# One quadrant product of each expert layer by seven products of quarters, sums kept in PSUM, and GpSimd's transfers moved and spaced

## The chip, the cores and the metric

The kernel runs on one core of a Trainium2 chip. The metric is device time in microseconds of one execution, the median of several runs. Engines are named as in the profile: PE is TensorE (PEld its weight loads), DVE VectorE, ACT ScalarE, POOL GpSimd, SP SyncE, which issues most DMAs.

## The reference

All is fp32. A thresholded attention over 8 batches, 8 heads, 576 positions, head size 64 is followed by a mixture of 8 experts (512 to 1024 to 512) in which a hash of the token's id chooses the one expert:

```python
scores = scale * np.matmul(q, k.transpose(0, 1, 3, 2))
thresh = np.max(scores, axis=-1, keepdims=True) - tau
scores = np.where(scores >= thresh, scores, -1e9)
scores = scores - np.max(scores, axis=-1, keepdims=True)
attn = np.exp(scores); attn /= np.sum(attn, axis=-1, keepdims=True) + 1e-09
x = np.matmul(attn, v)          # (B,H,S,D) -> (B*S, H*D) = (4608, 512)
expert_idx = token_ids * 2654435761 % 8
for e in range(8):
    xe = x[expert_idx == e]
    out[expert_idx == e] = np.maximum(xe @ w1[e], 0.0) @ w2[e]
```

## The kernel before

**Attention.** 32 pairs of heads, each in five steps (`n = 5 p + s`, s from 0 to 4), written out as one order for all engines in a loop over `n`. A step scores a block of queries (L235, PE), negates it and takes the row maximum (`ns`, L246, DVE), gets `thr` from it (L253, POOL), exponentiates (L260, ACT), masks the block of the step before (L271, DVE), turns the weights (L282, PE, copied by ACT at L303) and multiplies with v (L313, PE). In step 0 the output of a pair is turned back (`turn_o`), divided (`put_xm`, L352, DVE) and written to `x_scratch` by SP. Routing is done on the side: once every token has a slot, 36 scatters (`scatters`, L542, POOL) write the table of slots, one in each step but s = 1. From step n = 131 on `fetch_early` gathers rows of x for the first expert (L119, POOL), one at the head of each step 0 and one at the end of steps 3 and 4, 15 in all.

**Experts.** Expert e has `caps[e]` slots: 544 for the first, 576 for experts 1 to 4, 600 from 5 on. Each layer is a product of 2 x 2 blocks done by seven products in place of eight (`seven`): with a the weights and b the activations, c11 = a11 b11 + a12 b21, and five more products of sums (s1 to s4 of a, t1 to t4 of b) give c12, c21 and c22. The sums are made by DVE (`left`, `right`, L858 and L861). Layer 1 runs in two groups of columns (g = 0, 1), layer 2 in one. A product goes to one of four PSUM tiles of two banks in turn (`bank2`: names `sc` and `bank`), and DVE adds it to the running sums p1, u2, u3, u4 in SBUF; ACT copies p1 and applies the ReLU (L948). In layer 2 of all experts but the last the columns of w2 are dealt out (`dealt`): weights are read with a step of four elements. A matmul in fp32 is two instructions in the trace.

Calls of `side1` and `side2` between the products place other work: sums of the next layer and expert (`w2_work`, `h_work`, `x_work`), transposes of the next expert's x (`turns`, L1056, DVE, then 16 DMAs of SP into `xT`), the gathers for expert e + 2 (`fetch`), the loads of its weights (2 MB each, SP), and `put_squares`, which turns half of an expert's output into `o_q` (L1028, DVE) and writes it with 8 to 10 indirect DMAs (L1036, POOL). The last expert is written by `put_out` and `last_tile`. Engines take their instructions in the order written; a loop over overflow tokens at the end runs no round with these inputs.

Of the kernel before, what the change touches and what calls it, by code (L numbers as in the profile page):

```python
# [9 lines left out]
FP32 = mybir.dt.float32  # L10
# [10 lines left out]
def kernel(  # L21
# [122 lines left out]
    with tc.tile_pool(name="a_q", bufs=1) as a_q, \  # L144
# [543 lines left out]
        with tc.manual_schedule():  # L688
# [21 lines left out]
            for n in range(LAST + NS + 1):  # L710
                p, s = divmod(n, NS)
                m = n - 2
                if s == 0:
                    fetch_early(n)
# [85 lines left out]
                if s != 1 and placed:  # L800
                    next(scatter_pieces, None)
                if s > 2:
                    fetch_early(n)
# [23 lines left out]
    with tc.tile_pool(name="m_x", bufs=1) as m_x, \  # L827
         tc.tile_pool(name="m_o", bufs=3) as m_o, \
# [9 lines left out]
        o_end = m_x.tile([P, DIN], FP32, name="o_end")  # L838
# [4 lines left out]
        w2_s = m_s.tile([P, 3, FH, D2], FP32, name="w2_s")  # L843
        h_s = m_s.tile([P, 3, FH, CH], FP32, name="h_s")
        halves = [m_s.tile([P, 2, CH], FP32, name=n) for n in ("p1", "u2", "u3", "u4")]
# [3 lines left out]
        turn = [0]  # L849

        def bank2():
            turn[0] ^= 1
            if turn[0]:
                return ps_sc.tile([P, 2, 512], FP32, name="sc")
            return ps_m.tile([P, 2, 512], FP32, name="bank2")
# [31 lines left out]
        def w2_sums(e):  # L887
            t = triple(w2_s, 0, FH)
            return t if e == E - 1 else [dealt(x, C2) for x in t]
# [19 lines left out]
        def sums_w2(e):  # L909
            s1 = None  # L910
            if e == E - 1:
                spare = w_pool.tile([P, CO, F], FP32, name="w1_sb")
                s1 = w_tiles["s1"] = spare[:, :, 0:D2]
            return left(*w2_blocks(e, w_tiles[e, 2]), w2_sums(e), s1)
# [11 lines left out]
        def seven(a, a_s, b, b_s, m0, outs, relu, after):  # L926

            (a11, a12, s1, a22), (s2, s3, s4) = a, a_s
            (b11, t1, b21, b22), (t2, t3, t4) = b, b_s
            c11, c12, c21, c22 = outs  # L930
            n_k, width, dealt_out = a11.shape[1], b11.shape[2], len(a11.shape) == 4
            p1, u2, u3, u4 = (t[:, :, 0:width] for t in halves)

            def product(x, y):
                ps = bank2()
                for i in range(2):
                    c0 = m0 + P * i
                    for c in range(n_k):
                        lhsT = (x[:, c, :, i] if dealt_out else
                                x[:, c, c0:c0 + P])  # L940
                        nc.tensor.matmul(ps[:, i, 0:width], lhsT=lhsT, rhs=y[:, c],  # L941
                                         start=c == 0, stop=c == n_k - 1)
                return ps[:, :, 0:width]
# [253 lines left out]
```

## Time and profile before

| | |
|---|---|
| median of 6 runs | 938.46 us (936.81 to 942.33) |
| profiled execution | 940.78 us |
| its span, first to last instruction | 939.2 us |
| mean granted PE clock | 0.993 |
| attention / experts, about | 0 to 480 / 500 to 931 us |
| DMA traffic | 113.11 MB, mean 120 GB/s |

A group's line in the profile is: line, engine, operation, out<-in by the program's names, shapes, count | busy us, mean ns of one | idle time of the engine just before them and what ended it. "remote" or "another core or an unknown queue" stands where no instruction of the profile explains the end of a wait. PE's ends are modelled, since matmuls overlap; the distance between starts is what counts. Times of other kernels in this document stand against these runs.

### The profile page before, as it was taken

The page shows a single profiled execution, that of the slowest core. Times are in us where ns is not written, and L with a number is a line of the kernel's source. Part 1 is how long each engine was busy: PE and PEld are TensorE (multiplying, and loading weights), DVE is VectorE, ACT ScalarE, POOL GpSimd, SP SyncE. Part 2 cuts the span into 40 slices and gives each one's busy share as a digit, 9 for nine tenths or more (in the row PEclk, how much of TensorE's full clock was granted, in tenths as well). Part 3 has the DMA queues.
Part 4 walks back from the last instruction along what each step waited for, and adds up shares of the span by engine and source line. Part 5 has one row for each costly group of instructions (what it writes and reads, how often), then busy time and mean ns, then how long its engine had stood idle before and what let it go on. Part 6 is the DMA issues. An engine that isn't in the chain of part 4 may idle for free.

```text
span 939.2 us, 20725 instructions
## 1 busy us (share of the span) xinstructions
PE 914.6 (97%) x7495; PEld 664.4 (71%) x7495; DVE 757.9 (81%) x1654; ACT 457.2 (49%) x741; POOL 403.2 (43%) x528
## 2 busy tenths in 40 slices
PE   8999999999999999999999999999999999989996
PEld 4666666656666666565678887798888878768685
DVE  8999999999999999999756767768677786776551
ACT  6888888888888889888702020111102021020110
POOL 4233433456666532464325361716446171621602
PEclk9999999999999999999999999999999999999999
DMA  7355354454456667752103844363463626311101
GB/s 180 87 143 135 97 143 117 114 145 101 103 128 175 160 149 196 206 129 52 28 25 80 266 109 143 109 191 123 114 208 95 182 91 190 127 47 27 48 0 54
DMA packets 114775, 113.11 MB, mean 120 GB/s; under 512 B 32475, under 2 KB 89315, under 8 KB 114672
## 3 DMA queue, kind: packets, MB, share of 16 engines
q1 hardware_dynamic: 105168, 92.64, 37.4%
q0 software_dynamic: 9072, 18.91, 7.0%
q8 instruction: 61, 1.00, 0.5%
q14 instruction: 42, 0.34, 0.1%
q10 hardware_dynamic: 432, 0.21, 0.1%
HBM read 81.99 MB, written 21.44 MB: 110 GB/s over the span
## 4 chain that ended last, share of the span: by engine, by line
PE 68%; issue 18%; POOL 5%; DVE 2%; ACT 2%; DMA 2%; SPq 1%; another core or an unknown queue 1%; POOLq 0%; DVEq 0%; ACTq 0%
PE av L313 18%; PE sc L235 15%; PE tr L282 11%; PE bank L941 10%; PE sc L941 10%; POOL out_dram L1036 5%; PE sc L640 2%; PE av L282 1%; DMA xT<-xq 1%; ACT w L260 1%; ACT wT_b L303 1%; DMA k_sb<-in_k_dram 1%; POOL xg L119 1%; DVE ns L246 0%
## 5 line engine op out<-in xcount | busy, mean ns | idle before, releaser
L260 ACT ACTIVATE w<-ns,nmx 128x576 f32<-128x576 f32 x288 | 220.4, 776 | 29.6 <-DVE ns L246 29.1
L271 DVE SCALAR_TENSOR_TENSOR w<-ns,thr,w 128x576 f32<-128x576 f32 x288 | 225.4, 815 | 0.0
L1036 POOL DMA_INDIRECT out_dram<-o_q,qidx x127 | 136.9, 1078 | 198.6 <-DVE o_q L1028 159.9
L246 DVE TENSOR_SCALAR_CACHE_REDUCE ns<-sc 128x576 f32<-128x576 f32 x288 | 205.7, 747 | 8.8 <-PE sc L235 7.8
L253 POOL TENSOR_SCALAR thr<-nmx,drop 128x2 f32<-128x2 f32 (+1 forms) x160 | 103.1, 644 | 187.8 <-DVE ns L246 177.7
L235 PE MATMUL sc<-k_sb,q 64*128 64x288 f32 (+1 forms) x1280 | 178.9, 424 | 0.7 <-DVE drop L704 0.2
L282 PEld LDWEIGHTS tr<-ident,w 64*128 64x128 f32 x2624 | 105.5, 138 | 96.7 <-ACT wT_b L303 34.2
L282 PE MATMUL tr<-ident,w 64*128 64x64 f32 x2624 | 139.2, 230 | 7.2 <-ACT wT_b L303 4.3
L948 ACT ACTIVATE h<-h 128x576 f32<-128x576 f32 (+1 forms) x56 | 38.8, 693 | 172.0 <-DVE h L861 138.9
L235 PEld LDWEIGHTS sc<-k_sb,q 64*128 64x128 f32 (+1 forms) x1280 | 92.4, 177 | 23.7 <-DVE ns L246 9.6
L313 PE MATMUL av<-wT_a,v 128*64 128x320 f32 (+1 forms) x704 | 100.4, 418 | 0.2
L303 ACT COPY wT_a<-tr 128x512 f32<-128x512 f32 (+1 forms) x128 | 81.6, 638 | 20.9 <-PE tr L282 20.4
L303 ACT COPY wT_b<-tr 128x512 f32<-128x512 f32 (+1 forms) x128 | 81.3, 635 | 16.9 <-PE tr L282 9.6
L313 PE MATMUL av<-wT_b,v 128*64 128x256 f32 x640 | 83.2, 389 | 0.0
L313 PEld LDWEIGHTS av<-wT_a,v 128*64 128x64 f32 x704 | 43.7, 136 | 28.9 <-DVE xm L352 0.4
L951 ACT COPY p<-bank 128x576 f32<-128x576 f32 (+2 forms) x11 | 7.0, 632 | 98.7 <-PE bank L941 73.1
L313 PEld LDWEIGHTS av<-wT_b,v 128*64 128x64 f32 x640 | 40.2, 136 | 18.8 <-issue 0.7
L542 POOL DMA_INDIRECT slot_scratch<-tok,slot_i x36 | 45.2, 1255 | 9.8 <-issue 7.6
L941 PE MATMUL bank<-h,w_sb 128*128 128x288 f32 (+3 forms) x192 | 48.1, 404 | 0.0
L941 PE MATMUL sc<-h,w_sb 128*128 128x288 f32 (+3 forms) x192 | 47.7, 401 | 0.0
L941 PEld LDWEIGHTS bank<-h,w_sb 128*128 128x128 f32 x192 | 46.6, 300 | 0.5
L941 PEld LDWEIGHTS sc<-h,w_sb 128*128 128x128 f32 x192 | 45.9, 289 | 0.7
(197 smaller groups left out, 1314.7 us busy)
## 6 DMA issues: line engine op xcount, KB each, us to landing
w_sb<-in_moe_w_dram SPq DMA_DIRECT2D x16, 2048.0 KB
q<-in_q_dram SPq DMA_DIRECT2D x62, 288.0 KB
v<-in_v_dram SPq DMA_DIRECT2D x32, 256.0 KB
x_scratch<-xm SPq DMA_DIRECT2D x32, 256.0 KB
xT<-xq SPq DMA_DIRECT2D x84, 80.0 KB
k_sb<-in_k_dram SPq DMA_DIRECT2D x31, 144.0 KB
k_sb<-in_k_dram SPq DMA_DIRECT2D x32, 112.0 KB
x_scratch<-xg SPq DMA_DIRECT2D x9, 256.0 KB
```

The costliest lines, as they stand in the source:

```text
L235: nc.tensor.matmul(sc[out_rows, i, 0:S2], lhsT=q_sb[rows, h, q0:q1], rhs=k_sb[rows, h], start=True, stop=True)
L246: nc.vector.tensor_scalar(out=ns[:].rearrange("p (i s) -> p i s", i=2), in0=sc[:, :, 0:S2], scalar1=-1.0, scalar2=None, op0=ALU.mult, op1= ...
L253: nc.gpsimd.tensor_scalar(out=thr[:, 0:j + 1], in0=stats[n][0][:, 0:j + 1], scalar1=drop[:], scalar2=None, op0=ALU.add)
L260: nc.scalar.activation(w, nss[n, j][:], AF.Exp, bias=stats[n][0][:, j:j + 1], scale=-1.0)
L271: nc.vector.scalar_tensor_tensor(out=w, in0=nss.pop((n, j))[:], scalar=stats[n][1][:, j:j + 1], in1=w, op0=ALU.is_le, op1=ALU.mult, accum_ ...
L282: nc.tensor.transpose(dst[:, r, 64 * c:64 * c + 64], src[rows, c0:c0 + P], ident[rows, rows])
L303: nc.scalar.copy(dst, tr[:, :, 0:64 * n_c].rearrange("p r (c q) -> p r c q", c=n_c))
L313: nc.tensor.matmul(av[64 * j:64 * j + 64, g, c0:c1], lhsT=v_sb[:, c, 64 * j:64 * j + 64], rhs=wT[g][:, i, c0:c1], start=(c == 0), stop=stop)
L542: nc.gpsimd.indirect_dma_start(out=slot_dram[c % 2][:, :], out_offset=bass.IndirectOffsetOnAxis(ap=slot_i[:, c:c + 1], axis=0), in_=tok[:, ...
L941: nc.tensor.matmul(ps[:, i, 0:width], lhsT=lhsT, rhs=y[:, c], start=c == 0, stop=c == n_k - 1)
L948: nc.scalar.activation(c, c, AF.Relu)
L1036: inst = nc.gpsimd.indirect_dma_start(out=rows[:, :], out_offset=bass.IndirectOffsetOnAxis(ap=idx, axis=0), in_=o_sb, in_offset=None, boun ...
```

## The change

Three edits, all below in the diff.

1. In both layers of experts 1 to 7, a12 b21 is no longer computed as one block product but again by seven products of quarters (`Quarters`, operands from `w_quarters`, `b_quarters`, sums `wi_s`, `bi_s` made by `inner_w` and `inner_b`, w2's quarter copied to a packed tile by ACT in `copy_quarters`). Its products have half the columns, 144, 150 or 120.
2. The running sums p1, u2, u3 are accumulated in PSUM (`products` with `start=False`) on four fixed tiles (`banks`); ACT copies out the partial sums that are needed again. `Seven` and `Quarters` replace `seven`; `layer1` and `layer2` write the order of products out, and the side work is dealt to it by tables. `s4` of layer 2 is made in place. `put_squares(0, 0)` moves from layer 2 of expert 0 to layer 1 of expert 1, and the first half of later experts to the end of layer 2.
3. GpSimd's transfers: the scatters stand in attention steps 0 to 3 and the early gathers in 1 to 3; in the experts every write of `put_squares` and every gather after expert 1's is followed by `pause`, two copies of a 128 x 152 table.

The output tiles `o_sb` and `o_end` become the gather tiles `xg`. The diff, cut:

```diff
-                if s == 0:
-                    fetch_early(n)
...
-                if s != 1 and placed:
+                if s < NS - 1 and placed:
                     next(scatter_pieces, None)
-                if s > 2:
+                if 0 < s < NS - 1:
                     fetch_early(n)
                 if n == LAST:
...
-        w2_s = m_s.tile([P, 3, FH, D2], FP32, name="w2_s")
+        w2_s = m_s.tile([P, 2, FH, D2], FP32, name="w2_s")
+        w2_q = m_s.tile([P, 4, 2, P], FP32, name="w2_q")
-        halves = [m_s.tile([P, 2, CH], FP32, name=n) for n in ("p1", "u2", "u3", "u4")]
+        halves = [m_s.tile([P, 2, CH], FP32, name=n) for n in ("p1", "u2", "u3")]
+        wi_s = m_s.tile([P, 3, D2], FP32, name="wi_s")
+        bi_s = m_s.tile([P, 3, CH], FP32, name="bi_s")
+        quarters = [m_s.tile([P, CH], FP32, name=n) for n in ("q_p1", "q_u2", "q_p5")]
...
+        def bank2():
+            turn[0] += 1
+            return banks[(turn[0] - 1) % 4]
...
+            t = [w2_s[:, i] for i in range(2)]
+            if e == E - 1:
+                return [*t, w_tiles["s4"]]
+            return [*(dealt(x, C2) for x in t), w2_blocks(e, w_tiles[e, 2])[1]]
...
-        def seven(a, a_s, b, b_s, m0, outs, relu, after):
...
+        def products(ps, x, y, start, mid=None):
+            for i, lhsTs in enumerate(x):
+                for c, lhsT in enumerate(lhsTs):
+                    nc.tensor.matmul(ps[:, i], lhsT=lhsT, rhs=y[:, c], start=start and c == 0,
+                                     stop=c == len(lhsTs) - 1, skip_group_check=not start)
+                if i == 0 and mid:
+                    mid()
...
+            def first(self):
+                products(self.x, self.a[0], self.b[0], True)
+            def keep_p1(self):
+                nc.scalar.copy(self.p1, self.x)
+            def second(self, y):
+                y = y[:, :, 0:self.x.shape[2]]
+                products(y, self.a[1], self.b[2], True)
+                self.out(self.outs[0], y, self.p1)
+            def u2_sum(self):
+                products(self.x, self.a[4], self.b[4], False)
+                nc.scalar.copy(self.u2, self.x)
+            def s1_t1(self, keep):
+                products(self.z, self.a[2], self.b[1], True)
+                if keep:
+                    nc.scalar.copy(self.mid, self.z)
+            def u3_sum(self, keep):
+                products(self.x, self.a[5], self.b[5], False)
+                if keep:
+                    nc.scalar.copy(self.mid, self.x)
+            def c21(self):
+                products(self.x, self.a[3], self.b[6], False)
+                if self.relu:
+                    nc.scalar.activation(self.outs[2], self.x, AF.Relu)
+                else:
+                    nc.scalar.copy(self.outs[2], self.x)
+            def c12(self, mid=None):
+                products(self.z, self.a[6], self.b[3], False, mid)
+                self.out(self.outs[1], self.z, self.u2)
+            def c22(self, ps):
+                self.out(self.outs[3], ps, self.mid)
+            def c11(self, p1):
+                self.out(self.outs[0], p1, self.outs[0])
+        class Quarters:
...
+            def p1_p2(self):
+                products(self.x, self.a[0], self.b[0], True)
+                nc.scalar.copy(self.p1, self.x)
+                products(self.y, self.a[1], self.b[2], True)
+            def c11(self):
+                add(self.outs[0], self.y, self.p1)()
+            def p5_u2(self):
+                products(self.z, self.a[2], self.b[1], True)
+                nc.scalar.copy(self.p5, self.z)
+                products(self.x, self.a[4], self.b[4], False)
+                nc.scalar.copy(self.u2, self.x)
+            def c12_c22(self):
+                products(self.z, self.a[6], self.b[3], False)
+                add(self.outs[1], self.z, self.u2)()
+                products(self.x, self.a[5], self.b[5], False)
+                add(self.outs[3], self.x, self.p5)()
+            def c21(self):
+                products(self.x, self.a[3], self.b[6], False)
+                nc.scalar.copy(self.outs[2], self.x)
...
+        def copy_quarters(e):
+            w = w2_blocks(e, w_tiles[e, 2])[1]
+            nc.scalar.copy(w2_q[:].rearrange("p (i j) k m -> p i (j k) m", i=2),
+                           w.rearrange("p k m i -> p i k m"))
...
+            q = quarters_of(e, 1, *banks[1:])
+            g0, g1 = group(0, banks[0], banks[2]), group(1, banks[1], banks[3])
+            w_tiles.pop((e, 1))
+            g0.first()
+            g0.keep_p1()
+            side(0)
+            q.p1_p2()
+            q.c11()
+            g0.u2_sum()
+            side(1)
+            q.p5_u2()
+            g0.s1_t1(True)
+            side(2)
+            q.c12_c22()
+            side(3)
+            g0.u3_sum(False)
+            q.c21()
+            g0.c22(g0.x)
+            side(4)
+            g0.c12()
+            g0.c11(g0.p1)
+            g1.first()
+            g0.relus()
+            side(5)
+            g1.c11(g1.x)
+            g1.relus()
+            g0.c21()
+            side(6)
+            g1.u2_sum()
+            side(7)
+            g1.s1_t1(True)
+            side(8)
+            g1.u3_sum(False)
+            side(9)
+            g1.c22(g1.x)
+            g1.c12()
+            g1.relus()
+            side(10)
+            g1.c21()
...
+            o.first()
+            o.keep_p1()
+            if e == 0:
+                o.second(banks[0])
+                run(w2_first)
+                side(0)
+                o.u2_sum()
+                side(1)
+                o.s1_t1(True)
+                side(2)
+                o.u3_sum(False)
+                o.c22(o.x)
+                side(3)
+                o.c12()
+                side(4)
+                o.c21()
+                return
+            q = quarters_of(e, 2, *(banks[i][:, 0:1] for i in (2, 3, 3)))
+            q.p1_p2()
+            q.c11()
+            run(inner_b(second_blocks(e, 2)[1]), 4)
+            o.u2_sum()
+            q.p5_u2()
+            side(0)
+            o.u3_sum(True)
+            side(1)
+            q.c12_c22()
+            o.s1_t1(False)
+            side(2)
+            q.c21()
+            o.c11(o.p1)
+            o.c22(o.z)
+            o.c21()
+            side(3)
+            o.c12(lambda: side(4))
...
+        def pause():
+            for _ in range(2):
+                nc.gpsimd.tensor_copy(stok_odd[:], stok[:])
...
                 put_rows(o_q[i][:, s - s0].rearrange("p a c -> p (a c)"), qidx[:, e, s:s + 1],
                          rows=out_q)
+                pause()
...
+                if e > 1:
+                    pause()
...
+            w2_first = sums_w2(0)
+            run(w2_first, 3)
             fill(18)
-            late_h(lambda fo: (ps_sc.tile([P, 2, 512], FP32, name="sc") if fo in (2, 4) else
-                               ps_m.tile([P, 2, 512], FP32, name="bank2")))
+            late_h(late_tile)
+            for _ in range(2):
+                banks += [ps_sc.tile([P, 2, 512], FP32, name="sc"),
+                          ps_m.tile([P, 2, 512], FP32, name="bank2")]
...
-                    def side1(g, step):
-                        if g == 0:
-                            run(w2_work)
-                            if step == 0:
-                                put_squares(e - 1, 1)
-                        else:
-                            run(h_work)
-                        if step > 2:
-                            run(turns, 1 if g == 0 else 2)
+                    w2_work += inner_w(a, None if more else w_tiles["s1_q"])
+                    def side1(step):
+                        if step == 0 and e == 1:
+                            put_squares(0, 0)
+                        if step == (0 if e > 1 else 4):
+                            put_squares(e - 1, 1)
+                        if step == 2 and more:
+                            copy_quarters(e)
+                        run(w2_work, ((0, 1, 2, 0, 3, 1, 1, 0, 0, 0, 0) if e > 1 else
+                                      (0, 1, 2, 0, 0, 0, 1, 0, 1, 1, 0))[step])
+                        run(h_work, 2 if step in (8, 9) else 0)
+                        run(turns, ((0, 0, 0, 0, 0, 0, 1, 2, 1, 1, 1) if e > 1 else
+                                    (0, 0, 0, 0, 0, 1, 1, 1, 1, 2, 0))[step])
                     layer1(e, side1)
                     run(sums_h(e, 2, FH), 4)
-                x_work = (sums_w1(e + 1) + sums_x(e + 1)) if more else []
+                    run(w2_work, len(w2_work))
+                x_work = []
+                if more:
+                    a, b = second_blocks(e + 1, 1)
+                    x_work = [sums_w1(e + 1), sums_x(e + 1), inner_w(a), inner_b(b)]
+                    if e == 0:
+                        x_work[1:3] = x_work[2:0:-1]
+                    x_work = sum(x_work, [])
                 def side2(step):
                     if step == 0:
                         run(turns, len(turns))
-                    else:
-                        run(x_work, 2)
+                    run(x_work, ((1, 2, 3, 10, 0) if e else (2, 2, 0, 4, 8))[step])
                     if step == 2 and e + 2 < E:
                         fetch(e + 2)
                     if step == 4 and e + 2 < E:
                         load_w1(e + 2)
-                    if more and step == 3:
+                    if more and e and step == 4:
                         put_squares(e, 0)
```

## The prediction

> **What bounds the kernel now.** I read the page first, then busy time by stretch, then the timeline of the places where TensorE (PE) stood still, then the groups.
>
> ```profile
> PE 914.6 (97%) x7495; PEld 664.4 (71%) x7495; DVE 757.9 (81%) x1654; ACT 457.2 (49%) x741; POOL 403.2 (43%) x528
> PEclk9999999999999999999999999999999999999999
> ```
>
> PE is the bound almost everywhere, so two things can change the time: PE's own work, and the few places where it waits. Stretches show where those are (columns: us, then busy us and count for each engine, granted clock, DMA).
>
> ```profile
> 196.00:320.00 124.00, 122.60 (x1518) 76.17 (x1514) 119.98 (x330) 106.92 (x175) 82.85 (x104) 1.00 0.51 124
> 330.00:372.50 42.50, 42.50 (x538) 26.79 (x534) 42.12 (x119) 37.66 (x63) 13.71 (x25) 1.00 0.69 168
> 372.50:446.00 73.50, 70.11 (x864) 43.58 (x860) 68.86 (x191) 60.91 (x100) 38.39 (x53) 1.00 0.52 130
> 560.00:572.00 12.00, 10.15 (x35) 8.06 (x34) 5.41 (x8) 1.21 (x2) 0.20 (x1) 0.86 0.83 228
> 640.80:695.10 54.30, 54.30 (x226) 46.20 (x225) 39.76 (x48) 7.15 (x11) 25.68 (x25) 1.00 0.48 145
> 820.00:834.00 14.00, 11.02 (x36) 7.47 (x35) 9.17 (x13) 3.47 (x5) 6.12 (x7) 0.88 0.10 31
> 884.00:896.00 12.00, 9.73 (x31) 6.53 (x30) 5.68 (x9) 2.77 (x4) 4.48 (x5) 0.86 0.09 28
> ```
>
> The expert at 640.8 has no idle PE at all: 54.3 us of pure matmul. Attention without GpSimd transfers (330 to 372.5) has none either; with slot scatters (196 to 320) PE idles 1.4 us, with early gathers (372.5 to 446) 3.4 us. Three expert stretches idle 1.85, 2.98 and 2.27 us, and each then runs at a lower granted clock: 12 x 0.14, 14 x 0.12 and 12 x 0.14, about 1.7 us each. Together 7.1 + 5.1 = 12.2 us.
>
> Why PE stood still at 829, from the timeline (start, duration, engine, work, idle before and its releaser):
>
> ```profile
> 818.01 2.18 PE L941 MATMUL sc<-xT,w_s 128*128 128x300 f32 x8
> 829.47 2.20 PE L941 MATMUL sc<-x_s,w_s 128*128 128x300 f32 x4 [2.68 <-DVE h L861]
> ```
> ```profile
> 826.96 0.98 POOL L1036 DMA_INDIRECT out_dram<-o_q,qidx  x1 [0.30 <-issue]
> 828.63 0.78 DVE L861 TENSOR_TENSOR h<-sc,u 128x600 f32<-128x600 f32 x1 [3.63 <-remote]
> 830.16 0.66 ACT L951 COPY p<-bank 128x600 f32<-128x600 f32 x1
> ```
>
> The matmuls of that `sc` tile ended at 820.2, yet VectorE, idle for 3.63 us, added it only at 828.63; ScalarE copied a product that ended at 822.2 only at 830.16. Nothing else held them: PE's report of a finished product came 8 us late. GpSimd had sent an indirect DMA every 1.29 us since 802.8, and its last ends at 827.95. The stretches at 562 and 890 look alike. Lining up PE's semaphore updates with its matmuls over the whole trace, those that fall outside an indirect DMA come 0.02 to 0.05 us after the matmul, apart from backlog left by a burst; those inside are late in 20% of cases (scatters) to 42% (early gathers, expert bursts), by up to one DMA where DMAs stand alone and by 2 to 8 us late in a back-to-back burst.
>
> **The change, part by part.** Matmul prices:
>
> ```profile
> 696.95 2.10 PE L941 MATMUL bank<-xT,w_sb 128*128 128x288 f32 x8
> 698.89 2.10 PE L941 MATMUL sc<-x_s,w_s 128*128 128x288 f32 x8
> ```
> ```profile
> L990 PE MATMUL sc<-w_sb,h 128*120 128x128 f32 x16 | 1.9, 272 | 0.0
> ```
> ```profile
> L941 PEld LDWEIGHTS sc<-h,w_sb 128*128 128x128 f32 x44 | 10.9, 308 | 0.1
> L941 PEld LDWEIGHTS sc<-xT,w_sb 128*128 128x128 f32 x24 | 4.6, 190 | 1.3
> ```
>
> An fp32 matmul is two instructions. At 288 columns eight take 698.89 - 696.95 = 1.94 us, 242.5 ns each; at 128 columns sixteen take 1.91 us with the last one's 0.272 in it, so 109 ns each. Price follows columns with some 2.5 ns fixed: 144 columns 122 ns, 150 columns 127.
>
> *a12 b21.* Per layer 16 wide instructions (16 x 242.5 = 3.88 us) become 7 x 2 x 2 = 28 half-wide (3.43 us): 0.45 us less. Expert 0 keeps the old form; experts 1 to 6 have two such layers and 7 one, 13 x 0.45 = 5.9, plus 0.2 for the narrow last layer: -6.1 us. Against it: layer 2's strided weights load in 308 ns, plain ones in 190. The extra 118 hide under a 242 ns matmul but not under 122, so each switch from quarter to strided block (c12_c22 to s1_t1, c21 to c21; 12 in experts 1 to 6) shows 0 to 0.12 us; I take 0.10: +1.2. Net -4.9.
>
> *Sums in PSUM.* VectorE loses 12 adds of 0.755 us an expert and gains 6 half-size adds and 16 small sums (some 0.25 to 0.45 each, below the 0.755 of 576 elements): about 38 us of 54, as before. ScalarE rises from 7 to some 15 us. Neither is near a bound. But the four banks are now fixed, and PE accumulates onto a bank that ScalarE must first copy out. Three such hand-offs an expert have a cover of only 8 half-wide instructions, 0.98 us: keep_p1 to u2_sum in both layers, u2 to u3_sum in layer 2. The present hand-off: product's last instruction gives way at 807.91, ScalarE starts at 808.15, takes 0.66, and a released PE starts 0.05 us after (VectorE's add ends 829.42, PE starts 829.47): 0.95 us. Between 0 and 0.5 us each, as a late report would add; I take 0.10, the undisturbed rows being nearest: 21 x 0.1 = +2.1, and +1.5 for reports late by single DMAs (21 x 45% of time inside a DMA x some 30% late x 0.5). Elsewhere I walked both queues of an expert with these durations and found PE at least 0.7 us clear of ScalarE and VectorE; in expert 0 the transposes of x move behind one weight sum of 1.2 us, which may shift the present 0.4 us stall at 531 to 1 us.
>
> *Pacing.*
>
> ```profile
> L1036 POOL DMA_INDIRECT out_dram<-o_q,qidx x127 | 136.9, 1078 | 198.6 <-DVE o_q L1028 159.9 <-issue 36.8 <-DMA out_dram<-o_q,qidx 1.8
> L1049 POOL COPY mark<-h 1x1 f32<-1x1 f32 x5 | 1.5, 297 | 7.8 <-ACT h L664 7.8
> L215 POOL TENSOR_SCALAR k_sb<-k_sb,k_scale 128x576 f32<-128x576 f32 x31 | 24.2, 781 | 2.8
> ```
>
> Two copies of 128x152 follow each write and each gather after the first expert's. No such copy is in the trace: between 0.18 us (a 1x1 copy) and 0.78 (128x576); by size 0.35. So a DMA comes every 1.05 + 0.16 + 0.70 us plus waits of 0.3 to 0.5: 2.2 to 2.4 us instead of 1.29, with more than a microsecond free of descriptors in between, where scattered single DMAs in attention showed reports late by at most about one DMA. I take the three stalls as gone, -12.2 us (0 if not). Queued behind the copies on POOL are later writes, the gathers of expert e + 2, and nothing PE needs sooner than some 20 us. Load: 23 DMAs an expert x 2.2 to 2.4 = 51 to 55 us, of a new period of 53.9 (54.3 - 0.9 + 0.5). It just fits.
>
> A row on the port: one mark copy took 0.78 instead of 0.18 us, ending as VectorE's h sum ended; the next h sum, begun at once, took its usual 1.29. By the Trainium skill, "SBUF — State Buffer", "Who interferes with whom", a VectorE instruction with two SBUF inputs and a GpSimd one that reads SBUF exclude each other for a whole instruction, whoever starts first. By that rule alone, 46 copies could cost VectorE up to 46 x 0.35 = 16 us an expert, 38 + 16 = 54: a new bound. I weigh it as copies waiting, as the row shows.
>
> *Attention.* Scatters leave step 4 for step 1, early gathers move from steps 3, 4, 0 to 1, 2, 3. The 387 and 431 stalls follow gathers at 386.8 and 388.5, 1.7 us apart across the pair's end, and thr is queued behind the second. In steps 1 to 3 they stand 2.8 us apart. A gather in step 1 waits for the x_scratch write issued some 4 us into the pair; a thr of 0.7 us is queued behind it, used a step later. I take 2.4 of the 3.4 idle us and 0.5 of the 1.4 back (bounds +2 to -4.8): -2.9.
>
> *Sum*: 939.2 - 4.9 + 3.6 - 12.2 - 2.9 = 922.8 span; the profiled run took 940.78, 1.6 more than its span, giving 924.4; the median of the six is 2.3 below that run: **922 us**.
>
> The low clock, once more: it set in after 1.85 to 2.98 us of idling. The Trainium skill, "TensorE: Matmul & The Clock Gate", Part 1, gives an idle window of about 3.4 us as the condition; by it the stalls would cost 7.1, not 12.2. The row decides.
>
> **Rivals.** *Reports stay late*: the copies space the DMAs but PE's updates wait all the same. For: 42% late even for gathers 1.7 us apart. Against: no report is late outside DMAs but for a burst's backlog. Then 12.2 stays: 934. *GpSimd becomes the bound (slower)*: if copies wait for most of VectorE's sums, a DMA takes 2.9 us, 23 make 66.7 against 53.9; over five experts 64 us, less about 10 of slack, because VectorE's o_q transposes at the head of layer 1 wait for the last expert's writes, and the quarter's adds and PE stand behind them: 922 + 54 = 976. It eats the gain of 16 from 2.6 us on (23 x 2.6 = 59.8; 5 x 5.9 - 10 = 19). For: VectorE is busy 73% of an expert. Against: the one mark copy got in between two sums. *The tight hand-offs stall*: 21 x 0.5 to 1.2 us as reports come late, 930 to 945.
>
> **How the numbers follow.** Forecast (912 to 929) 0.62; reports stay late 0.15; GpSimd bound 0.12; hand-offs 0.11. A change of 0.3%, 2.8 us, is about what a measurement of this kernel can tell from none. Faster: 0.62, 0.10 of the second, 0.04 of the last; same 0.02 and 0.03; slower 0.03, 0.12, 0.04. Low end: 922 less the other 1.9 of attention, 3.6 of hand-offs, 1.2 of loads, 0.4 at 531 and 3 for the spread of the runs (936.81 to 942.33) is 912; the high end 942 takes in the second rival and most of the hand-offs, leaving GpSimd as the bound outside.
>
> **What would show it.** Right: no stretch of an expert below clock 1.00; DVE starting within 0.1 us of PE's product; POOL DMAs 2.2 to 2.4 us apart; an undisturbed expert of 53 to 54 us; pairs after 372 of 14 us. Wrong: DVE idle with "remote" as releaser, o_q transposes waiting for DMAs, PE waiting for p or u copies by more than 0.2 us, 144-column instructions above 125 ns.

## The result and the profile after

The changed kernel took 935.8 us (median; 932.9 to 938.38) beside 937.88 for the kernel before (931.29 to 944.36) in runs that alternated on one chip: a ratio of 0.9973, 95% interval 0.996 to 0.9986. The ratio makes 2.5 us less, the two medians 2.1, where 16 were forecast. 935.8 lies above the 912 to 929 of the forecast itself, though inside the range that reaches to 942; and 0.27% is less than the 0.3% called "no change".

The page of the profiled execution (span 932.8 us, 6.4 less than before's):

```profile
PE 907.6 (97%) x7663; PEld 672.2 (72%) x7663; DVE 760.6 (82%) x1720; ACT 514.1 (55%) x848; POOL 559.9 (60%) x842
...
POOL 4233432456766632456125588887878878888873
PEclk9999999999999999999999999999989989999999
```

PE still is the bound on average, but POOL, 43% before, shows 7 or 8 tenths in all but the last slice from 560 us on, and the clock drops in two slices. Busy time by stretch (start and end, length, then busy time and count of PE, PEld, DVE, ACT, POOL, then granted clock, DMA share, GB/s):

```profile
196.00:320.00 124.00, 123.07 (x1532) 77.46 (x1528) 121.68 (x336) 107.03 (x175) 83.75 (x106) 1.00 0.53 127
372.50:446.00 73.50, 72.63 (x892) 45.29 (x890) 70.28 (x196) 63.11 (x103) 37.84 (x55) 1.00 0.51 130
560.38:614.14 53.76, 53.76 (x250) 47.02 (x249) 41.24 (x59) 15.42 (x27) 45.27 (x63) 1.00 0.48 145
614.14:667.95 53.81, 53.81 (x250) 47.00 (x249) 40.87 (x59) 15.49 (x27) 42.38 (x61) 1.00 0.46 142
684.00:704.00 20.00, 13.51 (x60) 10.93 (x60) 9.91 (x10) 4.41 (x7) 15.52 (x25) 0.83 0.56 168
744.00:766.00 22.00, 17.53 (x73) 14.33 (x73) 12.23 (x16) 5.64 (x8) 17.50 (x28) 0.84 0.52 163
```

Attention idles 0.93 + 0.87 us where it idled 1.40 + 3.39. The three old stalls are gone, and two experts run without a gap at 53.8 us (54.3 before). But two new stretches idle 6.49 and 4.47 us, at a low clock. The first, from the timeline (start, duration, engine, work, and in brackets the idle time before it and what ended that):

```profile
684.20 2.29 DVE L1239 STREAM_TRANSPOSE o_q<-oT 128x1152 f32<-128x1152 f32 x1
...
685.24 2.10 PE L937 MATMUL sc<-xT,w_sb 128*128 128x288 f32 x8
...
685.53 0.37 SPq L140 DMA_DIRECT2D w_sb<-in_moe_w_dram  x1
...
690.62 0.98 POOL L1248 DMA_INDIRECT out_dram<-o_q,qidx  x1 [0.43 <-issue]
690.64 0.65 PE L937 MATMUL bank<-bi_s,wi_s 128*128 128x144 f32 x4
...
691.59 0.71 POOL L1233 COPY stok_odd<-stok 128x152 int32<-128x152 int32 x2
...
695.23 2.22 DVE L1239 STREAM_TRANSPOSE o_q<-oT 128x1152 f32<-128x1152 f32 x1 [8.15 <-DMA out_dram<-o_q,qidx]
...
697.30 0.43 DVE L864 TENSOR_TENSOR h<-sc,q_p 128x288 f32<-128x288 f32 x1
...
697.66 1.20 DVE L861 TENSOR_TENSOR w_s<-w_sb 128x1024 f32<-128x1024 f32 x1
...
697.78 4.10 PE L937 MATMUL sc<-xT,w_sb 128*128 128x288 f32 x8 [6.49 <-DVE h L864]
698.61 1.68 POOL L1233 COPY stok_odd<-stok 128x152 int32<-128x152 int32 x2
698.89 1.23 DVE L864 TENSOR_TENSOR w_sb<-w_sb 128x1024 f32<-128x1024 f32 x1
```

Read it backwards. PE at 697.78 needs the bank that VectorE's small sum frees (q.c11, 697.30). That sum stands behind the second o_q transpose. VectorE was free for it at 687.08 and waited 8.15 us for the last write of the expert before, issued only at 690.62. That write took until 695.05 to land, among the 2 MB weight load issued at 685.53. Then eight matmuls took 4.10 us instead of 2.10, at half clock. This is the sign that the prediction named as wrong: o_q transposes waiting for DMAs.

So the wait has two parts: the write was issued 3.54 us after VectorE was free, and took 4.43 us to land. In the second stretch only the landing is left. VectorE was free at 749.58, the last write had been issued at 748.91, and beside the weight load issued at 747.97 it took 6.86 us to land. The two landings from the chain of work that ended last, then the second wait from the timeline:

```profile
690.62 4.43 DMA out_dram<-o_q,qidx
748.91 6.86 DMA out_dram<-o_q,qidx
```
```profile
755.85 2.22 DVE L1239 STREAM_TRANSPOSE o_q<-oT 128x1152 f32<-128x1152 f32 x1 [6.27 <-DMA out_dram<-o_q,qidx]
...
758.43 4.37 PE L937 MATMUL sc<-xT,w_sb 128*128 128x300 f32 x8 [4.47 <-DVE h L864]
```

Why the first write was late, and why the second left no time to land, from the groups:

```profile
L1233 POOL COPY stok_odd<-stok 128x152 int32<-128x152 int32 x314 | 145.5, 463 | 10.0
L1248 POOL DMA_INDIRECT out_dram<-o_q,qidx x127 | 144.3, 1136 | 56.2 <-issue 45.5 <-DVE h L864 9.7 <-DVE oT L864 1.0
```

A copy takes 0.463 us on average (median 0.32, longest 1.38), not the 0.35 taken. What holds the long ones can be read off the trace: all 79 copies of over 0.5 us began while a VectorE sum ran and ended 0.16 to 0.18 us after a sum had ended, like the pair at 698.61, whose end at 700.29 is 0.17 us after that of the sum begun at 698.89. The first gathers of successive experts are issued at 574.7, 632.7, 692.8, 751.1 and 808.5, so a round of 23 DMAs takes 58.4 us, 2.54 each, against an expert of 53.8. From expert to expert the last write comes closer to the transpose that needs it, until a stall sets it back.

### The profile page after: what moved, and what is told of

It is laid out like the page before. It is cut to its first block, busy times and chain, and to the rows that moved or that the text cites. A ratio compares the mean times of both kernels' runs of the same rounds, so it can differ in the third digit from the quotient of the medians.

```text
span 932.8 us, 21618 instructions
## 1 busy us (share of the span) xinstructions
PE 907.6 (97%) x7663; PEld 672.2 (72%) x7663; DVE 760.6 (82%) x1720; ACT 514.1 (55%) x848; POOL 559.9 (60%) x842
## 4 chain that ended last, share of the span: by engine, by line
PE 69%; POOL 15%; issue 6%; DVE 3%; ACT 3%; DMA 2%; SPq 1%; POOLq 0%; DVEq 0%; ACTq 0%
PE av L313 17%; PE sc L235 15%; PE sc L937 12%; PE tr L282 11%; PE bank L937 9%; POOL out_dram L1248 8%; POOL stok_odd L1233 6%; PE sc L640 2%; PE av L282 2%; ACT w L260 1%; DMA out_dram<-o_q,qidx 1%; SPq L1278 1%; ACT wT_a L303 1%; POOL xg L119 1%; DMA k_sb<-in_k_dram 1%
## 5 line engine op out<-in xcount | busy, mean ns | idle before, releaser
L253 POOL TENSOR_SCALAR thr<-nmx,drop 128x2 f32<-128x2 f32 (+1 forms) x160 | 98.2, 614 | 174.6 <-DVE ns L246 163.1
L235 PE MATMUL sc<-k_sb,q 64*128 64x288 f32 (+1 forms) x1280 | 178.9, 422 | 1.1 <-DVE ns L246 0.7
L1248 POOL DMA_INDIRECT out_dram<-o_q,qidx x127 | 144.3, 1136 | 56.2 <-issue 45.5
L1233 POOL COPY stok_odd<-stok 128x152 int32<-128x152 int32 x314 | 145.5, 463 | 10.0
L235 PEld LDWEIGHTS sc<-k_sb,q 64*128 64x128 f32 (+1 forms) x1280 | 92.2, 177 | 24.3 <-DVE ns L246 10.9
L937 PE MATMUL bank<-h,w_sb 128*128 128x288 f32 (+4 forms) x248 | 62.0, 402 | 0.0
L937 PEld LDWEIGHTS bank<-h,w_sb 128*128 128x128 f32 x248 | 58.7, 290 | 0.5
L937 PE MATMUL sc<-h_s,w_s 128*128 128x288 f32 (+2 forms) x224 | 56.6, 406 | 0.0
L119 POOL DMA_INDIRECT xg<-x_scratch,gidx_x x35 | 44.1, 1261 | 19.4 <-issue 8.2
L961 ACT ACTIVATE h<-h 128x576 f32<-128x576 f32 (+1 forms) x42 | 29.0, 693 | 41.2 <-DVE h L864 39.5
```

Of the source, the lines that this page charges most:

```text
L119: nc.gpsimd.indirect_dma_start(out=dst, out_offset=None, in_=src, in_offset=bass.IndirectOffsetOnAxis(ap=idx, axis=0), bounds_check=src.sh ...
L235: nc.tensor.matmul(sc[out_rows, i, 0:S2], lhsT=q_sb[rows, h, q0:q1], rhs=k_sb[rows, h], start=True, stop=True)
L253: nc.gpsimd.tensor_scalar(out=thr[:, 0:j + 1], in0=stats[n][0][:, 0:j + 1], scalar1=drop[:], scalar2=None, op0=ALU.add)
L937: nc.tensor.matmul(ps[:, i], lhsT=lhsT, rhs=y[:, c], start=start and c == 0, stop=c == len(lhsTs) - 1, skip_group_check=not start)
L1233: nc.gpsimd.tensor_copy(stok_odd[:], stok[:])
L1248: inst = nc.gpsimd.indirect_dma_start(out=rows[:, :], out_offset=bass.IndirectOffsetOnAxis(ap=idx, axis=0), in_=o_sb, in_offset=None, boun ...
```

## The experiments

Theory: pacing makes PE's reports punctual, as forecast, but its queue is longer than an expert; VectorE's o_q transposes meet the lag, and PE stands. Rivals: the second copy is needed to keep the reports punctual, the tight hand-offs are what costs, or the placement of the transpose decides and not the queue's length.

The runs fell on several chips, and these differ. Lining up PE's semaphore updates with its products, as in the prediction, I call a chip *late* if updates come more than 0.3 us after products, *punctual* if none does. A is the chip of the result. The kernel before was profiled on chip A alone; elsewhere the kind is read off the kernels tried there (on C and F, where all were paced, off their attention). Each chip was used on one occasion, so a chip and its occasion can't be told apart.

| chip | before, us | kind |
|---|---|---|
| A | 937.88 | late |
| B, D | 918.36, 918.86 | punctual |
| C, E, F | 930.79, 930.31, 929.77 | late |

A ratio below is the time of the run's kernel over that of the kernel before on the same chip, with its 95% interval. Besides it I give two lengths of each profile: the start of the last score matmul (L235), which ends attention, and the *expert part*, from the first matmul of the seven products to the first of the last tile. Before on chip A: 458.5 and 421.9. After: 454.1 and 420.3.

**On chip B: one copy, no copy, pacing alone, old attention steps.**

```diff
-            for _ in range(2):
-                nc.gpsimd.tensor_copy(stok_odd[:], stok[:])
+            nc.gpsimd.tensor_copy(stok_odd[:], stok[:])
```


> The changed kernel with one paced copy behind each indirect DMA instead of two. Theory (GpSimd's paced queue is longer than an expert: 23 DMAs at 2.5 us make 58 us against 53.8, VectorE's o_q transposes wait for its writes, and PE behind them stands 6.5 and 4.5 us and then runs at half clock): a DMA now comes every 1.7 to 2.0 us, 23 make 39 to 46 us, no o_q transpose waits for a DMA, both stalls and their half clock (about 17 us) go, reports stay punctual: span 914 to 921. Rival (the second copy is what keeps PE's reports punctual): reports 0.5 to 1.5 us late at the tight hand-offs and one or more stalls of 2 us come back: span 925 to 940.

The ratio was 0.9974 (0.9965 to 0.9984), the expert part 404.1 us, as the theory had it. DMAs come some 1.7 us apart at the median, and no transpose waits.

```diff
-            for _ in range(2):
-                nc.gpsimd.tensor_copy(stok_odd[:], stok[:])
+            return
```


> The changed kernel without any paced copy. Theory (reports come late in back-to-back bursts of indirect DMAs, and the copies are what cured it): DMAs 1.29 us apart, VectorE and ScalarE idle on PE's reports by up to 8 us as in the kernel before, two to four stalls of 2 to 3 us with half clock in the experts, more at the tight hand-offs than before; no o_q transpose waits for a DMA: span 928 to 945. Rival (the attention steps and the smaller product did all that was gained, and the copies only cost): no late report above 0.5 us in the experts, span 914 to 921.

The ratio was 0.998 (0.997 to 0.9989), the expert part 404.1 us, with no late report: the rival's number, but on a chip whose kernel before took 918 us and so has no stall to cure. Of pacing this says nothing; it had to be repeated.

```diff
             for s in range(s0, s1):
                 put_rows(o_q[i][:, s - s0].rearrange("p a c -> p (a c)"), qidx[:, e, s:s + 1],
                          rows=out_q)
+                pause()
...
                 gather(x_dram, xg_bufs[k][:], gidx_x[:, e, k:k + 1])
+                if e > 1:
+                    pause()
```


> The kernel before, with two copies behind each indirect DMA of the experts and nothing else. Theory: the three stalls on late reports go (-12), but 23 DMAs of 2.5 us make 58 us against a period of 54.3, so o_q transposes wait for DMAs from the fourth expert on, with one or two stalls of 4 to 7 us and half clock (+10 to +17): span 936 to 945. Rival (the queue's overrun hurts only through the new order of the changed kernel's layer 1, where the quarter's sums stand behind the o_q transpose): no stall, span 925 to 929.

(`pause` is the changed kernel's two copies.) The ratio was 0.9991 (0.9982 to 1.0), the expert part 407.9 us, without a wait at o_q, though a round also takes 57 to 58 us. The rival about placement is right here. In this kernel the second o_q transpose follows the first after 11.3 us (569.42, 580.70), in the changed one after 2.9 (576.6, 579.5): the change had moved it 8.4 us towards the lag. From the last write to the moment when VectorE is free for the transpose there are 18.9 us in the second expert here, and still 5.7 and 3.4 in the last two; in the changed kernel 7.4, then 2.8, then minus 3.5.

```diff
                 m = n - 2
+                if s == 0:
+                    fetch_early(n)
...
-                if s < NS - 1 and placed:
+                if s != 1 and placed:
...
-                if 0 < s < NS - 1:
+                if s > 2:
                     fetch_early(n)
```


> The changed kernel with scatters and early gathers in the attention steps of the kernel before. Both theories: attention from 196 to 446 idles 4.8 us instead of 1.8, so 2 to 4 us slower than the changed kernel, span 935 to 937; unless the later start shifts the two stalls. If the placement is worth nothing: span 932 to 934.

The ratio was 1.0135 (1.0119 to 1.015): with two copies the expert part is 420.5 us, as on chip A, though not one report is late here. The two stalls belong to the queue and what waits for it, not to late reports. Attention ended at 449.9 us against 452.4 and 453.3 in the two runs above with the new steps: without late reports the old placement is the better one. The stretch 372.5 to 446, first in the kernel before with two copies (old steps), then in the changed one without copies (new):

```profile
372.50:446.00 73.50, 73.50 (x910) 45.98 (x912) 73.05 (x204) 64.29 (x105) 43.61 (x58) 1.00 0.50 129
```
```profile
372.50:446.00 73.50, 72.03 (x888) 44.86 (x886) 69.77 (x195) 62.62 (x102) 37.46 (x57) 1.00 0.49 125
```

The old steps do not idle at all, the new ones 1.47 us.

**On chip C: where the stall comes from.**

```diff
-                        if step == (0 if e > 1 else 4):
+                        if step == (3 if e > 1 else 4):
                             put_squares(e - 1, 1)
```


> The changed kernel with VectorE's second o_q transpose of an expert three steps later in layer 1 (behind the quarter's c12 and c22 sums, some 9 us), as far behind the first one as in the kernel before; GpSimd's queue, its copies and their order are untouched. Theory (the stall is not the paced queue's length alone, 58 us against 53.8, but that this transpose was moved ahead by some 8 us and so meets the queue's lag): lag grows to some 15 us and stays covered, no o_q transpose waits for a DMA, no stall: 14 to 18 us below the changed kernel on the same chip. Rival (the queue's length alone decides): the stalls only come later in layer 1, less than 6 us below the changed kernel.

It took 927.44 us beside 935.45 of the changed kernel, 8.0 less, with an expert part of 412.9 us. This lies between theory and rival: placement is worth half. The lag does not stay covered: from the last write to the transpose there are 15.0 us in the second expert, then 10.4, 2.9 and minus 0.1:

```profile
754.63 2.27 DVE L1239 STREAM_TRANSPOSE o_q<-oT 128x1152 f32<-128x1152 f32 x1 [3.42 <-DMA out_dram<-o_q,qidx]
...
761.96 2.29 PE L937 MATMUL bank<-x_s,w_s 128*128 128x300 f32 x8 [2.11 <-DVE h L864]
```

So both were needed for the full stall, too long a queue and the earlier transpose.

```diff
-                nc.gpsimd.tensor_copy(stok_odd[:], stok[:])
+                nc.gpsimd.memset(stok_odd[:], 0)
```


> The changed kernel with its two pacing copies per DMA made two memsets of the same tile, which read no SBUF. Theory that copies are stretched because they read SBUF while VectorE's two-input sums hold it: the memsets keep one length (none over 0.5 us), a DMA comes every 2.0 to 2.2 us, 23 make 46 to 50 us, both stalls go: 14 to 18 us below the changed kernel on the same chip. Rival (anything that GpSimd does to SBUF is held off by VectorE's sums): memsets of 1 us and more remain, DMAs 2.4 to 2.6 us apart, stalls remain, within 5 us of the changed kernel.

The ratio was 0.9878 (0.9845 to 0.9911), 16.2 us below the changed kernel, with an expert part of 404.9 us, no late report in the experts and no wait at o_q. The memsets are not stretched (from the groups on POOL, as the repeat on chip F has them):

```profile
L1233 POOL MEMSET stok_odd<- 128x152 int32 x314 | 72.8, 232 | 9.2
```

They take 0.232 us each and none over 0.27, beside the same VectorE sums. The copy, which reads SBUF, is held off; the memset, which only writes it, is not.

```diff
                 gather(x_dram, xg_bufs[k][:], gidx_x[:, e, k:k + 1])
-                if e > 1:
-                    pause()
```


> The changed kernel with pacing copies behind the writes alone, none behind the gathers. Theory: 18 x 2.53 + 5 x 1.5 = 53 us against 53.8, the queue just keeps up, at most one short wait: 12 to 18 us below the changed kernel on the same chip, if the five bare gathers make no late report; on a chip that has late reports one or two stalls of 1 to 3 us in layer 2 or at the head of layer 1 may come instead.

The ratio was 0.9886 (0.9854 to 0.9917), 15.6 us below the changed kernel, with an expert part of 404.0 us. A round is 53.8 us (571.8, 625.6, 679.3, 733.1), 53 had been reckoned, and that suffices.

> The changed kernel itself, unaltered, beside the others on their chip. If this chip shows the kernel before without late reports, as the last four runs did (mean granted clock 0.997 to 0.999, 918 us): two or three stalls of 4 to 7 us at the o_q transposes are left with nothing gained against them, 926 to 932 us, 0.8 to 1.5% slower than before. If it shows late reports (before at 931 to 944 us): 932 to 938 us, as measured.

The ratio was 1.0047 (1.0028 to 1.0067), with waits of 8.29 and 6.84 us at the transposes and an expert part of 420.6 us. 935.45 us agrees with chip A's 935.8; it is the kernel before that differs from chip to chip, so the ratio does too.

**On chip D, which proved punctual**, four kernels for the same question: the changed kernel without copies, with one copy and with two memsets, and the kernel before with two memsets.

> The changed kernel without any pacing, once more, since the first time fell on a chip whose kernel before shows no late report. Theory (pacing earns what the late reports cost, where there are any): if the kernel before takes over 925 us here, PE's updates are late by up to 8 us in the experts' bursts, the stalls are there, and this kernel is 5 to 15 us slower than the one with two memsets. Rival (the new placement of transposes and the smaller products took the stalls away by themselves): within 2 us of the one with two memsets, no expert stall. If the kernel before takes 918 us here, all four are expected at 915 to 919 us.

> The changed kernel with one copy per DMA, once more, for a chip with late reports. Theory: DMAs 1.6 to 2.3 us apart leave 0.6 us and more between them, reports late by at most 0.6 us, no o_q wait, no stall above 1 us in the experts: within 2 us of the one with two memsets. Rival (two copies' distance is needed): reports late by 1 us and more, one or more stalls, 3 to 12 us slower than with two memsets.

> The kernel before with two memsets behind each indirect DMA of the experts, nothing else changed. Theory: on a chip with late reports the expert stalls go and the attention ones stay: 8 to 13 us below the kernel before; on a chip without them nothing changes (within 1 us). Rival (pacing needs the new order of sums to pay): less than 4 us below the kernel before on a chip with late reports.

> The changed kernel with two memsets per DMA, beside the others on their chip. Theory: 916 to 921 us on any chip, since neither late reports nor the queue's length reach PE: 0.98 to 0.99 of the kernel before where that takes over 925 us, 0.998 to 1.0 where that takes 918.

The ratios were 0.9977, 0.9978, 0.9997 and 0.9985 (each within 0.0010), the expert parts 404.0, 404.2, 407.9 and 404.8 us, without a late report. Here pacing is worth nothing, and costs nothing while the queue keeps up.

**On chip E, late**, the first and third of these again.

> The changed kernel without any pacing. On a chip where the kernel before takes over 925 us, theory (pacing earns): reports up to 8 us late in the experts' bursts, two to four stalls with half clock, 0.992 to 1.01 of the kernel before, against the 0.988 measured with two memsets. Rival (the rest of the change removed the stalls): 0.985 to 0.990, no expert stall. On a chip with 918 us: 0.997 to 0.999, as measured twice.

The ratio was 1.0674 (1.0621 to 1.0727): 997.72 us (984.89 to 1000.69), far worse than expected. The profile is of the slowest of its six runs (span 999.1, expert part 485.3 us; the mean clock of all six is 0.97, which goes with their stalls). Some 30 reports in the experts are late, by up to 13.8 us. One place on its timeline:

```profile
671.21 2.21 PE L937 MATMUL bank<-x_s,w_s 128*128 128x288 f32 x8 [1.52 <-DVE h L864]
...
673.26 2.10 PE L937 MATMUL bank<-xT,w_sb 128*128 128x288 f32 x8
...
678.95 0.98 POOL L1247 DMA_INDIRECT out_dram<-o_q,qidx  x1 [0.30 <-issue]
680.24 1.04 POOL L119 DMA_INDIRECT xg<-x_scratch,gidx_x  x1 [0.30 <-issue]
...
685.51 1.00 POOL L119 DMA_INDIRECT xg<-x_scratch,gidx_x  x1 [0.30 <-issue]
685.59 0.64 ACT L979 COPY u<-bank 128x576 f32<-128x576 f32 x1 [8.92 <-issue]
686.28 3.62 PE L937 MATMUL bank<-x_s,w_s 128*128 128x288 f32 x8 [10.92 <-issue]
```

The first of these products (u2_sum of the second group) ended at 673.4. ScalarE copied it out only at 685.59, after an unbroken row of DMAs some 1.3 us apart, and PE, which accumulates u3_sum on that very bank, stood for 10.92 us behind the product after it. The rival, that the rest of the change removed the stalls, is out: the new product without pacing is far more exposed to late reports than the old one (930.31 us on this chip).

> The kernel before with two memsets behind each indirect DMA of the experts, nothing else changed. On a chip where the kernel before takes over 925 us, theory: expert stalls go, attention ones stay, 0.986 to 0.993 of the kernel before. Rival: 0.995 to 1.0. On a chip with 918 us: within 0.1%, as measured.

The ratio was 0.9945 (0.9924 to 0.9967), the expert part 408.4 us with no late report in it; some 27 remain in attention. The expert stalls are gone as the theory had it, but the ratio lies 0.15% above the theory's range, and its interval reaches into the rival's. The range was reckoned from chip A, where the kernel before takes 938 us and not 930; here pacing alone earns 5.7 us.

**On chip F, late**: two memsets with the old attention steps, one copy, and two memsets.

> The changed kernel with two memsets per DMA, and scatters and early gathers in the attention steps of the kernel before. Theory: on a chip with late reports 2 to 4 us slower than two memsets with the new steps (the idle time of TensorE from 196 to 446 is 4.8 us with the old steps, 1.8 with the new). On a chip without late reports the old steps idle by nothing and the new ones by up to 1.8 us: 1 to 2 us faster than two memsets with the new steps, 914 to 916 us. Rival (placement is worth the same on any chip): 2 to 4 us slower on both.

> The changed kernel with one copy per DMA. On a chip with late reports, theory (any gap of half a microsecond between DMAs lets the reports through): within 3 us of two memsets, no stall above 1 us in the experts. Rival (two copies' distance is needed): reports late by 1 us and more where two DMAs stand less than 1.7 us apart, 5 to 40 us slower than two memsets. On a chip without late reports: within 1 us of two memsets.

> The changed kernel with two memsets per DMA, beside the other two on their chip: 916 to 921 us on any chip, 0.985 to 0.99 of the kernel before where that takes over 925 us, 0.998 to 1.0 where it takes 918.

The ratios were 0.9908 (0.9887 to 0.9929), 0.9865 (0.9843 to 0.9888) and 0.988 (0.9856 to 0.9903), the expert parts 404.8, 404.3 and 404.5 us; attention ended at 457.8 us with the old steps, 455.6 and 452.7 with the new. The new steps earn 4.0 us on a late chip by the medians with two memsets (921.49 and 917.45), 2 to 5 by these profiles, and cost some 2 in attention on a punctual one: the rival, the same worth everywhere, is out. One copy (917.86 us) and two memsets (917.45) can't be told apart; the kernel before took 929.77 here. Both are faster than the kernel before on chip D too, and far below the 935 us that the changed kernel took on A and C. The page with one copy:

```profile
PE 903.2 (98%) x7663; PEld 669.3 (73%) x7663; DVE 759.1 (83%) x1720; ACT 514.0 (56%) x848; POOL 487.5 (53%) x685
...
PEclk9999999999999999999999999999999999999999
```

Not tried: deeper o_q buffers, which would take the wait from the transposes and leave the queue as it is; and another time for the weight load, beside which the last writes landed late.

## Why the forecast was wrong, step by step

The sum for the pair on chip A, with what the runs put in each place:

| term | forecast, us | measured, us | from |
|---|---|---|---|
| attention steps | -2.9 | -4.4 in this pair; -3.0 over the late chips | last score 458.5 to 454.1; means 457.6 (3 profiles, old) and 454.6 (8, new) |
| three expert stalls | -12.2 | -13.5 | expert part 421.9 before (chip A), 408.4 paced by memsets (E) |
| product by quarters | -4.9 + 3.6 | -3.9 | 408.4 (E) to 404.5 (F), both with two memsets |
| queue over its period | 0 | +15.8 | 404.5 (F) to 420.3 (A); on chip C alone 404.9 to 420.6 |
| sum | -16.4 | -6.0 | span fell by 6.4 |

The expert rows set profiles of different chips side by side. That is sound as far as stall-free expert parts agree between chips, and they do: 404.0 to 404.9 in all ten with the new product, 407.9 to 408.4 in all three with the old. The size of the three stalls does not carry over: it is that of chip A's one profile, and on chip E pacing alone earned 5.7 us in all.

**The failed step is the pacing's load, "23 DMAs an expert x 2.2 to 2.4 = 51 to 55 us, of a new period of 53.9 (54.3 - 0.9 + 0.5). It just fits."** 2.2 to 2.4 is what the median came to (2.28). The queue's length goes by the mean, 2.54, and 23 x 2.54 = 58.4. The price was 1.05 for the DMA, 0.70 for two copies, 0.16 between them and 0.3 to 0.5 of waits; over the four rounds the DMA took 1.15, two copies 0.94, and GpSimd was idle for 0.46. The idle time uses up the waits that were allowed, so what is left over is the copies' 0.24 and the DMA's 0.10. With copies at the 0.35 that was priced by size, and the rest as measured, a round would be 53.0 us, by this estimate, and would still fit. The copy's median matches that price; its tail, copies held off by VectorE's sums up to 1.38 us, does not. I had weighed "copies waiting" from the one mark copy that took 0.78 instead of 0.18, and then priced every copy by its size.

A second thing was put at nothing: how long the last write takes to land. Beside the weight load it took 4.43 and 6.86 us. A lead of 18.9 us from write to transpose covers that; the minus 3.5 and 0.7 us that were left at the two stalls did not.

**"The GpSimd becomes the bound" was the right rival with its mechanism right, though not its 976 us**: o_q transposes wait for the last expert's writes, and the quarter's sums and PE stand behind them. Its formula, fed the measured pitch, gives 5 x (58.4 - 53.9) - 10 = 12.5 us; PE stood 6.49 + 4.47 = 11.0, and the low clock behind the stalls, which the rival had not priced, added 2.0 + 2.4 (4.10 instead of 2.10 us for eight matmuls, and 4.37 and 0.92 instead of 2.18 and 0.67). It got 0.12. Its threshold, 2.6 us, was close: at 2.54 the queue took 15.8 of the 21.8 us that the other three rows gained. That the result fell inside the range up to 942 is luck: that end was set for the other two rivals, and this one was meant to lie outside it. What I did not cost at all was the second transpose's move 8.4 us ahead, which the order of VectorE's instructions shows and which by the run with the later transpose (412.9 of 420.6 to 404.9) is worth half.

**Reports stay late**: not so. With one copy, two copies or two memsets no report in the experts was over 0.3 us late on a late chip, and without pacing some 30 were.

**The tight hand-offs**: with paced DMAs they cost less than the 3.6 taken. Against the distance that its columns call for, matmul starts come some 3 us late in all over the unstalled expert part, against 0.4 to 0.8 in the paced old one. This includes the switches of weights; 4.8 had been reckoned for both. Without pacing the kernel lost 6.7% on chip E, with stalls like the one shown, far beyond the 930 to 945 given to this rival.

**The port rule.** The Trainium skill, "SBUF — State Buffer", "Who interferes with whom", has a VectorE instruction with two SBUF inputs and a GpSimd one that reads SBUF exclude each other for a whole instruction, whichever starts first; by it VectorE might have lost up to 16 us an expert, by an estimate from that rule. Measured, VectorE's whole busy time is 760.6 us with two copies and 755.0 with two memsets (chip F): 5.6 us in the whole kernel, beside 44 us that the 314 copies took over their median. Most of the waiting was done by the copies, as the row had shown, and the harm came from that.

**The low clock** set in again at stalls of 4.5 to 6.5 us; one stall of 2.11 us in the run with the later transpose (761.96) left the granted clock at 1.00, another of 2.01 (876.72) brought 0.86 over twelve microseconds. The length of one stall alone does not decide it.

## What to carry to other kernels

Price a queue by the mean of its instructions under load, not by the median or by size, and compare the sum with the period whenever something that reuses its buffers waits on it; add the time that its last transfer takes to land beside whatever else is loading. "Just fits" with an error of a tenth is a coin toss. When a change reorders an engine, look for each waiting instruction that moved nearer to what it waits for, even if nothing of it was edited. Filler instructions for pacing should touch as little as possible: a memset, or one copy in place of two, gave the same punctuality here without the stall.

## What the runs showed of the hardware that I had not expected

The same kernel took 918.4 and 918.9 us on two chips and 930 to 938 on four others, and what goes with it is PE's semaphore updates: some 30 late ones in the experts of the kernel before on chip A, by up to 8 us, and none on chips B and D, where the changed kernel without copies sent its indirect DMAs in such bursts too. So the changed kernel with two memsets is worth 11.6 and 12.3 us on C and F and 1.4 on D, and the new attention steps are worth minus 2.3 on B and D (attention ends at 450.5 with the old steps and 452.8 with the new, means of 3 and 5 profiles). Why the chips differ stays open; no run here tells it.

A write's landing goes with what else is under way: 4.43 and 6.86 us from its issue while a 2 MB weight load ran (690.62 and 748.91), against 3.27 behind such a load (751.33 in the run with the later transpose). In the kernel before with two memsets on chip D, the six writes issued within 6 us of a weight load's issue took 4.3 to 7.2 us, and the 40 others whose landing the trace tells 2.2 to 3.1.
